# A decode block rebuilt: one load queue, two heads per 4 MB load, a quarter of K on TensorE, the norm folded behind the FFN

## The chip, the cores and the metric

One core of a Trainium2 chip runs the kernel. It has TensorE (PE, matrix products), VectorE (DVE), ScalarE (ACT), GpSimd (POOL) and SyncE (SP), each with an instruction stream of its own, and 16 DMA engines that carry data between HBM and the core's SBUF. TensorE writes to PSUM. A load is issued by an engine's queue; here SP and ACT issue loads. An instruction can wait for semaphores, and whatever stands behind it on that engine waits too. The metric is the device time in microseconds.

## The reference

One token of each of two sequences passes through attention over a cache of 8192 positions with 32 heads of 128, and then through a gated feed-forward part (FFN). Nearly all bytes are K and V: 64 heads of 2 MB each, twice.

```python
B, D, Hq, Sk, Dh, F = 2, 512, 32, 8192, 128, 1376      # all bf16
q = (layernorm(x) @ wq)                                  # per head: 128 values
p = softmax((q . k_cache[b, h]) * Dh ** -0.5)            # 8192 scores per head
o = p @ v_cache[b, h]
h = x + o.reshape(B, 1, Hq * Dh) @ wo
gate, up = layernorm(h) @ W_gate, layernorm(h) @ W_up
out = h + (gate * (gate > 0) * up) @ W_down
```

## The kernel before

A head's K is loaded as `[128 partitions, 64, 128]`: partition p holds the 64 positions 64p to 64p + 63, 16 KB in a row. The loop `for i in range(NH)` runs over the 64 heads; K and V have three buffers each (`kt`, `vt`, `NB = 3`).

For each head VectorE multiplies K by q, which lies copied in all partitions (`prod`, line 327), then adds halves of the 128 products, from 128 to 64, 32, 16 and 8 wide (`tb` and `prod` in turn, line 349), and reduces the last 8 (line 358): 64 scores per partition. ScalarE takes the exponential and its sum (line 363). TensorE multiplies V by the exponentials, 64 matmuls with one column each (line 377). Softmax's division is left to the end.

SP issues the K loads (`dma_k`, line 194), each after the multiply that frees its buffer. ACT issues the V loads (`dma_v`, line 200), each after the PV matmuls that free its buffer. SP's queue also carries x (line 247, in pieces of 2 bytes), wq in eight chunks of 1 KB rows (line 187), wo (behind the K load of head 8, in 1 KB rows), and at the end the FFN's weights into the freed K and V buffers.

q comes in groups of four heads: four matmuls with 512 columns (line 213), whose stationary operand is the normalized x copied along 128 columns, and a copy by ScalarE (line 226).

After the last head comes one chain: the sums of the exponentials (line 399), their reciprocals, spread to all partitions by a matmul (407), the scaling of O (413), the output projection, 128 matmuls (422), the addition of x (427), the second norm with a square root on ScalarE (431 to 453), gate and up (464, 470), their product (475 to 483), W_down (494), the addition, a transpose (506) and the store (511).

Of the kernel before, what the change touches and what calls it, by code (L numbers as in the profile page):

```python
# [6 lines left out]
F32 = mybir.dt.float32  # L7
# [6 lines left out]
class EngChain:  # L14

    def __init__(self, eng, sem):
        self.eng = eng
        self.sem = sem
        self.count = 0
        self.pending = False  # L20

    def wait(self):
        if self.pending:
            self.eng.wait_ge(self.sem, self.count)
            self.pending = False

    def run(self, inst):
        inst.then_inc(self.sem, 1)
        self.count += 1
        self.pending = True  # L30
        return inst


def bass_sequential_preLN__gqa_block_cached__glu_gated_reglu__decode_kernel(
# [13 lines left out]
    _, Hkv, Sk, Dh = A_k_cache.shape  # L48
    Hq = A_wq.shape[1] // Dh
    assert Hq == Hkv  # L50
    assert Dh == 128
    assert D % 128 == 0
    DC = D // 128
    J = Sk // 128
    assert Sk % 128 == 0 and J >= 2 and (J & (J - 1)) == 0
    F = B_W_gate.shape[1]
    FC = (F + 127) // 128
    NH = B * Hq
    inv_sqrt_dh = 1.0 / math.sqrt(Dh)
    eps = 1e-5  # L60
    qdim = Hq * Dh
    GH = 4 if Hq % 4 == 0 else Hq
    NGB = Hq // GH
    NG = B * NGB
    GW = GH * Dh
    assert GW <= 512
    NB = 3

    with ExitStack() as es:
# [3 lines left out]
        sem_x = S("x")  # L73
        sem_wo = S("wo")
        sem_wgu = S("wgu")
        sem_wd = S("wd")
        sem_prep = S("prep")
        sem_stats = S("stats")
        sem_lnx = S("lnx")
        sem_qps = S("qps")  # L80
        sem_qcopied = S("qcopied")
        kdone = [S(f"kdone{k}") for k in range(NB)]
        vdone = [S(f"vdone{k}") for k in range(NB)]
        multdone = S("multdone")
        sready = S("sready")
        expdone = S("expdone")
        pvdone = S("pvdone")
        sem_ident0 = S("ident0")
        sem_ident = S("ident")
        sem_z = S("ztok")  # L90
        sem_zinv = S("zinv")
        sem_zb = S("zb")
        sem_osb = S("osb")
        sem_attn = S("attn")
        sem_hprep = S("hprep")
        sem_hstats = S("hstats")
        sem_hn = S("hn")
        sem_gu = S("gu")
        sem_hd = S("hd")
        sem_y = S("ysem")  # L100
        sem_h2 = S("h2sem")
        sem_rows = S("rowsem")
        sem_rowsb = S("rowsbsem")
        osem = S("osem")
        dvesem = S("dvechain")
        sem_sq1a = S("sq1a")
        sem_sq1b = S("sq1b")
        sem_sq2a = S("sq2a")
        sem_sq2b = S("sq2b")

        dve = EngChain(nc.vector, dvesem)
        actsem = S("actchain")
        actc = EngChain(nc.scalar, actsem)

        kt = [es.enter_context(nc.sbuf_tensor(f"kt{i}", [128, J, Dh], BF16)) for i in range(NB)]
        vt = [es.enter_context(nc.sbuf_tensor(f"vt{i}", [128, J, Dh], BF16)) for i in range(NB)]
        wq_sb = es.enter_context(nc.sbuf_tensor("wq_sb", [128, DC, qdim], BF16))
        xrep = es.enter_context(nc.sbuf_tensor("xrep", [128, B * DC, 128], BF16))
        q_grp = [es.enter_context(nc.sbuf_tensor(f"qgrp{i}", [128, GW], BF16)) for i in range(2)]
        wo_sb = es.enter_context(nc.sbuf_tensor("wo_sb", [128, Hq, D], BF16))  # L120
        ones_f32 = es.enter_context(nc.sbuf_tensor("ones_f32", [128, 128], F32))
        ident_f32 = es.enter_context(nc.sbuf_tensor("ident_f32", [128, 128], F32))
        xT = es.enter_context(nc.sbuf_tensor("xT", [128, DC, B], BF16))
        xT_f = es.enter_context(nc.sbuf_tensor("xT_f", [128, DC * B], F32))
        xsq = es.enter_context(nc.sbuf_tensor("xsq", [128, DC * B], F32))
        sumb = es.enter_context(nc.sbuf_tensor("sumb", [128, B], F32))
        sumq = es.enter_context(nc.sbuf_tensor("sumq", [128, B], F32))
        mean = es.enter_context(nc.sbuf_tensor("mean", [128, B], F32))
        msq = es.enter_context(nc.sbuf_tensor("msq", [128, B], F32))
        var = es.enter_context(nc.sbuf_tensor("var", [128, B], F32))  # L130
        rstd = es.enter_context(nc.sbuf_tensor("rstd", [128, B], F32))
        vareps = es.enter_context(nc.sbuf_tensor("vareps", [128, B], F32))
        sqv = es.enter_context(nc.sbuf_tensor("sqv", [128, B], F32))
        lnxT = es.enter_context(nc.sbuf_tensor("lnxT", [128, DC, B], BF16))
        hT_f = es.enter_context(nc.sbuf_tensor("hT_f", [128, DC * B], F32))
        hsq = es.enter_context(nc.sbuf_tensor("hsq", [128, DC * B], F32))
        hnT = es.enter_context(nc.sbuf_tensor("hnT", [128, DC, B], BF16))
        hd = es.enter_context(nc.sbuf_tensor("hd", [128, FC * B], BF16))
        h2T_f = es.enter_context(nc.sbuf_tensor("h2T_f", [128, DC * B], F32))
        rows_sb = es.enter_context(nc.sbuf_tensor("rows_sb", [DC * B, 128], BF16))  # L140
        zinv = es.enter_context(nc.sbuf_tensor("zinv", [1, NH], F32))
        ZP = es.enter_context(nc.sbuf_tensor("ZP", [128, NH], F32))
        zb_sb = es.enter_context(nc.sbuf_tensor("zb_sb", [128, NH], F32))
        u_sb = es.enter_context(nc.sbuf_tensor("u_sb", [128, FC * B], F32))
        O_sb = es.enter_context(nc.sbuf_tensor("O_sb", [128, Hq, B], BF16))
        prod = es.enter_context(nc.sbuf_tensor("prod", [128, J, Dh], BF16))
        tb1 = es.enter_context(nc.sbuf_tensor("tb1", [128, J * 64], BF16))
        scores = [es.enter_context(nc.sbuf_tensor(f"scores{i}", [128, J], F32)) for i in range(2)]
        e_t = [es.enter_context(nc.sbuf_tensor(f"e{i}", [128, J], BF16)) for i in range(2)]

        if DC * F <= J * Dh and FC * D <= J * Dh and NH >= 3:
            alias_w = True
            pstride = kt[0][:].ap[0]
            wg_view = bass.AP(kt[(NH - 3) % NB], 0, [[pstride[0], 128], [F, DC], [1, F]])
            wu_view = bass.AP(kt[(NH - 2) % NB], 0, [[pstride[0], 128], [F, DC], [1, F]])
            wd_view = bass.AP(vt[(NH - 3) % NB], 0, [[pstride[0], 128], [D, FC], [1, D]])
        else:
            alias_w = False
            wg_t = es.enter_context(nc.sbuf_tensor("wg_sb", [128, DC, F], BF16))
            wu_t = es.enter_context(nc.sbuf_tensor("wu_sb", [128, DC, F], BF16))  # L160
            wd_t = es.enter_context(nc.sbuf_tensor("wd_sb", [128, FC, D], BF16))
            wg_view = wg_t[:]
            wu_view = wu_t[:]
            wd_view = wd_t[:]

        qps = es.enter_context(nc.psum_tensor("qps", [128, 2 * 512], F32))
        work = es.enter_context(nc.psum_tensor("work", [128, 512], F32))
        O_ps = work[:, 0:NH]
        zrow_ps = work[0:1, 64:64 + NH]
        zb_ps = work[:, 128:128 + NH]  # L170
        msum_ps = work[:, 192:192 + DC * B]
        e2_ps = work[:, 200:200 + DC * B]
        attnT_ps = work[:, 208:208 + DC * B]
        hsum_ps = work[:, 216:216 + DC * B]
        hsq_ps = work[:, 224:224 + DC * B]
        g_ps = work[:, 232:232 + FC * B]
        u_ps = work[:, 254:254 + FC * B]
        yT_ps = work[:, 276:276 + DC * B]
        rows_ps = work[0:DC * B, 288:288 + 128]

        NWQ = NGB
        sem_wq = [S(f"wq{k}") for k in range(NWQ)]
        nfull = F // 128
        frem = F - nfull * 128

        def dma_wq_chunk(k):
            return nc.sync.dma_start(  # L187
                wq_sb[:, :, k * GW:(k + 1) * GW],
                A_wq[:, k * GW:(k + 1) * GW].rearrange("(c p) n -> p c n", p=128),
            ).then_inc(sem_wq[k], 16)  # L190

        def dma_k(i):
            b, h = divmod(i, Hq)
            return nc.sync.dma_start(  # L194
                kt[i % NB][:], A_k_cache[b, h].rearrange("(p j) d -> p j d", p=128)
            ).then_inc(kdone[i % NB], 16)

        def dma_v(i):
            b, h = divmod(i, Hq)
            return nc.scalar.dma_start(  # L200
# [3 lines left out]
        def emit_q_group_pe(g):  # L204
# [4 lines left out]
            if g >= 2:  # L209
                nc.tensor.wait_ge(sem_qcopied, g - 1)  # L210
# [335 lines left out]
```

## Time and profile before

| what | value |
|---|---|
| time, median of 3 runs | 710.17 us (710.09 to 710.2) |
| profiled execution: span | 708.4 us |
| first multiply of a head starts | 27.43 us |
| the last head's scores are done | 688.70 us |
| VectorE busy | 630.6 us, 424 instructions |
| TensorE busy | 158.7 us, 4433 matmuls |
| ScalarE busy | 34.4 us |
| read from HBM | 281.05 MB |

The span runs from the first instruction to the last of one profiled execution; the time of a run contains a little more around it. The profile page cuts the span into 40 slices and gives for each the busy tenths of the engines, the share of the 16 DMA engines and the GB/s. Its groups list instructions by line, with the count, the busy time in all, the mean of one in ns, and the idle time before them with what ended it. In an order of time, each line has the start, the duration, the engine, the line and the operation.

### The profile page before, as it was taken

To read this page: it belongs to the slowest core of one execution; us is meant where nothing else is said; L and a number is where in the kernel's file an instruction comes from. 1 tells how busy PE (TensorE), PEld (TensorE's weight loads), DVE (VectorE), ACT (ScalarE), POOL (GpSimd) and SP (SyncE) were. 2 spreads that over 40 slices of the span, in tenths; PEclk is the share of its full clock that TensorE was granted. 3 is DMA by queue.
4 is the path that set the end of the run, shared out by engine and by line. 5 is a ranking of instruction groups with operands and counts; after the bars stand their busy time and mean duration, and the time that the engine had idled before them with its cause. 6 is when DMAs were issued, how large, how long until landed. Compare 5 with 4: busy or idle time off the path is not lost.

```text
span 708.4 us, 9878 instructions
## 1 busy us (share of the span) xinstructions
PE 158.7 (22%) x4433; PEld 130.2 (18%) x4433; DVE 630.6 (89%) x424; ACT 34.4 (5%) x149; POOL 0.7 (0%) x6
## 2 busy tenths in 40 slices
PE   0221322011323132212322132122322232112215
PEld 0111222011222122212221122112221222112215
DVE  0679998299999999999999999999999999999982
ACT  0100000000000000000000000000000000000010
POOL 0000000000000000000000000000000000000000
DMA  9999999999999999999999999999999999999940
GB/s 345 367 426 427 425 417 392 423 396 384 426 424 421 421 418 427 409 409 424 420 425 422 422 413 424 422 412 423 428 427 409 420 424 417 420 417 416 401 162 3
DMA packets 30346, 281.70 MB, mean 398 GB/s; under 512 B 3328, under 2 KB 12896, under 8 KB 13920
## 3 DMA queue, kind: packets, MB, share of 16 engines
q1 hardware_dynamic: 21088, 146.84, 49.9%
q10 hardware_dynamic: 9216, 134.22, 46.1%
q8 instruction: 35, 0.57, 0.3%
q14 instruction: 7, 0.06, 0.0%
HBM read 281.05 MB, written 0.00 MB: 397 GB/s over the span
## 4 chain that ended last, share of the span: by engine, by line
DVE 84%; DMA 8%; SPq 4%; PE 2%; issue 2%; DVEq 0%; ACT 0%
DVE prod L327 38%; DVE tb L349 25%; DVE prod L349 14%; DMA kt<-in_A_k_cache_dram 8%; DVE scores L358 6%; SPq L194 2%; SPq L187 2%; PE work L422 1%; PE work L377 0%; PE work L464 0%; DVEq L323 0%; PE work L470 0%; PE work L494 0%; SPq L247 0%; ACT e L363 0%
## 5 line engine op out<-in xcount | busy, mean ns | idle before, releaser
L327 DVE TENSOR_TENSOR prod<-kt,qgrp 128x8192 bf16<-128x8192 bf16 x64 | 283.3, 4426 | 29.5 <-DMA kt<-in_A_k_cache_dram 20.8
L377 PE MATMUL work<-e,vt 128*128 128x1 bf16 x4096 | 119.5, 165 | 517.7 <-ACT e L363 517.7
L377 PEld LDWEIGHTS work<-e,vt 128*128 128x128 bf16 x4096 | 114.3, 104 | 535.2 <-ACT e L363 535.2
L349 DVE TENSOR_TENSOR tb<-prod 128x4096 bf16<-128x4096 bf16 (+1 forms) x128 | 190.9, 1491 | 4.4
L349 DVE TENSOR_TENSOR prod<-tb 128x2048 bf16<-128x2048 bf16 (+1 forms) x128 | 105.6, 825 | 4.4
L363 ACT ACTIVATE e<-scores 128x64 bf16<-128x64 f32 x64 | 16.4, 256 | 630.8 <-DVE scores L358 630.8
L358 DVE TENSOR_REDUCE scores<-prod 128x64 f32<-128x512 bf16 x64 | 43.9, 686 | 2.2
L213 PE MATMUL qps<-wq_sb,xrep 128*128 128x512 bf16 x64 | 29.9, 623 | 4.4 <-DVEq L303 3.3
L262 DVE CAST xT_f<-xT 128x8 f32<-128x8 bf16 x1 | 0.2, 172 | 19.0 <-DMA xT<-in_A_x_dram 19.0
L363 ACT ACTIVATION_READ_ACCUMULATOR e<-scores 128x1 f32 x64 | 11.9, 186 | 0.0
L213 PEld LDWEIGHTS qps<-wq_sb,xrep 128*128 128x128 bf16 x64 | 6.9, 128 | 14.2 <-issue 8.8
L226 ACT ACTIVATE qgrp<-qps 128x512 bf16<-128x512 f32 x16 | 9.3, 579 | 4.0 <-PE qps L213 4.0
L268 PE MATMUL work<-xT_f,ones_f 128*128 128x8 f32 x2 | 0.6, 372 | 20.4 <-DVE xsq L264 20.4
L268 PEld LDWEIGHTS work<-xT_f,ones_f 128*128 128x128 f32 x2 | 0.5, 310 | 20.4 <-DVE xsq L264 20.4
L422 PE MATMUL work<-O_sb,wo_sb 128*128 128x2 bf16 x128 | 3.6, 165 | 0.6 <-DVEq L416 0.6
L422 PEld LDWEIGHTS work<-O_sb,wo_sb 128*128 128x128 bf16 x128 | 3.5, 104 | 0.8 <-DVEq L416 0.8
L427 DVE TENSOR_TENSOR hT_f<-work,xT_f 128x8 f32<-128x8 f32 x1 | 0.2, 167 | 3.7 <-PE work L422 3.7
L475 DVE COPY u_sb<-work 128x20 f32<-128x20 f32 x1 | 0.2, 178 | 3.1 <-PE work L470 3.1
L403 DVE RECIPROCAL zinv<-work 1x64 f32<-1x64 f32 x1 | 0.5, 547 | 2.6 <-PE work L399 2.6
L464 PE MATMUL work<-hnT,kt 128*128 128x2 bf16 (+1 forms) x44 | 1.5, 170 | 2.1 <-DVEq L457 2.1
L464 PEld LDWEIGHTS work<-hnT,kt 128*128 128x128 bf16 (+1 forms) x44 | 1.5, 112 | 2.2 <-DVEq L457 2.2
L470 PE MATMUL work<-hnT,kt 128*128 128x2 bf16 (+1 forms) x44 | 1.5, 170 | 0.0
(53 smaller groups left out, 21.0 us busy)
## 6 DMA issues: line engine op xcount, KB each, us to landing
vt<-in_A_v_cache_dram ACTq DMA_DIRECT2D x64, 2048.0 KB, 13.0
kt<-in_A_k_cache_dram SPq DMA_DIRECT2D x64, 2048.0 KB, 13.6
wq_sb<-in_A_wq_dram SPq DMA_DIRECT2D x8, 512.0 KB, 11.4
wo_sb<-in_A_wo_dram SPq DMA_DIRECT2D x1, 4096.0 KB, 41.8
kt<-in_B_W_gate_dram SPq DMA_DIRECT2D x1, 1376.0 KB, 10.9
kt<-in_B_W_up_dram SPq DMA_DIRECT2D x1, 1376.0 KB, 6.5
vt<-in_B_W_down_dram SPq DMA_DIRECT2D x1, 1280.0 KB, 9.0
vt<-in_B_W_down_dram SPq DMA_DIRECT2D x1, 96.0 KB, 9.2
```

The costliest lines, as they stand in the source:

```text
L187: return nc.sync.dma_start(wq_sb[:, :, k * GW:(k + 1) * GW], A_wq[:, k * GW:(k + 1) * GW].rearrange("(c p) n -> p c n", p=128),).then_inc( ...
L194: return nc.sync.dma_start(kt[i % NB][:], A_k_cache[b, h].rearrange("(p j) d -> p j d", p=128)).then_inc(kdone[i % NB], 16)
L213: last = nc.tensor.matmul(qps[:, slot * 512:slot * 512 + GW], lhsT=xrep[:, b_g * DC + c, :], rhs=wq_sb[:, c, col0:col0 + GW], start=(c == ...
L226: actc.run(nc.scalar.activation(out=q_grp[slot][:], in_=qps[:, slot * 512:slot * 512 + GW], func=ACT.Copy))
L327: nc.vector.tensor_tensor(out=prod[:], in0=kt[buf][:], in1=qb, op=ALU.mult).then_inc(multdone, 1)
L349: dve.run(nc.vector.tensor_tensor(out=out_ap, in0=cur_in[:, :, 0:half], in1=cur_in[:, :, half:cur_w], op=ALU.add))
L358: nc.vector.tensor_reduce(out=scores[par][:], in_=cur_in, axis=AX.X, op=ALU.add).then_inc(sready, 1)
L363: nc.scalar.activation(out=e_t[par][:], in_=scores[par][:], func=ACT.Exp, scale=inv_sqrt_dh, accum_out=ZP[:, col:col + 1]).then_inc(expdon ...
L377: last = nc.tensor.matmul(O_ps[:, col:col + 1], lhsT=vt[buf][:, j, :], rhs=e_t[par][:, j:j + 1], start=(j == 0), stop=(j == NJ - 1))
L422: last = nc.tensor.matmul(attnT_ps[:, ncx * B:(ncx + 1) * B], lhsT=wo_sb[:, h, ncx * 128:(ncx + 1) * 128], rhs=O_sb[:, h, :], start=(h == ...
L464: last = nc.tensor.matmul(g_ps[0:fw, fc * B:(fc + 1) * B], lhsT=wg_view[:, c, fc * 128:fc * 128 + fw], rhs=hnT[:, c, :], start=(c == 0), s ...
L470: last = nc.tensor.matmul(u_ps[0:fw, fc * B:(fc + 1) * B], lhsT=wu_view[:, c, fc * 128:fc * 128 + fw], rhs=hnT[:, c, :], start=(c == 0), s ...
```

## The change

The kernel's body is written anew; what is computed stays. The parts:

- **Loads.** K and V come two heads at a time (heads 2hp and 2hp + 1 of one sequence), 4 MB each, 32 KB in a row per partition; 64 partitions belong to each head. There are four slots of 4 MB: K in 0 and 2, V in 1 and 3. wq comes whole into slot 3, in 32 KB rows. All loads but x are issued by SP, in one order. wo is issued behind V of pair 16, the FFN's weights go into K's slot of pair 30, ahead of V of pair 31, which comes in four pieces.
- **Scores.** Of a pair's 128 columns, VectorE takes two chunks of 48 in the same way as before. The other 32 are turned by TensorE (four groups of eight transposes), copied to SBUF by ScalarE, and multiplied with q, two columns for the two heads.
- **PV.** 128 matmuls of two columns for a pair: `e_t` has a column for each head, zero in the other head's partitions.
- **q.** 128 matmuls give q with the head's dimension on the partitions; eight rounds of a copy, four matmuls with the identity and a ScalarE copy spread it over the partitions.
- **Output projection.** The sums of the exponentials and the scaling come in batches of pairs 0-7, 8-15, 16-23, 24-30 and 31. 24 heads are projected at pair 27, the rest at the end.
- **Second norm.** Since the gate keeps its sign under a positive factor, `1/(var + eps)` is applied once behind W_down; there is no square root. The output is stored with the partitions outermost.

The removed lines are those of the kernel above. The core of the new ones:

```diff
+    NP = B * H // 2
+    J = 2 * Sk // 128
+    GT = 8
+    NG = 4
+    JP = NG * GT
+    NCH = 2
+    JC = (J - JP) // NCH
...
+        def load(s, dst, src, eng=sp):
+            slot_cnt[s] += 16
+            eng.eng.dma_start(dst, src).then_inc(slot_sem[s], 16)
+            return (slot_sem[s], slot_cnt[s])
+
+        def kv(cache, p):
+            hp, b = divmod(p, B)
+            return cache[b, 2 * hp:2 * hp + 2].rearrange("h (p j) d -> (h p) (j d)", p=64)
...
+                nc.scalar.dma_start(x_row[:], A_x[:, 0]).then_inc(sem_x, 16)
+                t_wq = load(3, slot[3][:], A_wq.rearrange("(p c) n -> p (c n)", c=DC))
+                t_k, t_v = {}, {}
+                t_k[0] = load(0, slot[0][:], kv(A_k_cache, 0))
+                t_v[0] = load(1, slot[1][:], kv(A_v_cache, 0))
+                t_k[1] = load(2, slot[2][:], kv(A_k_cache, 1))
...
+                sp.wait(t_q)
+                t_v[1] = load(3, slot[3][:], kv(A_v_cache, 1))
...
+                def score_group(p, g):
+                    n = p * NG + g
+                    pe.wait(t_ev[n])
+                    if g == 0 and p >= 2:
+                        pe.wait(t_exp[p - 2][0])
+                    for k in range(GT):
+                        jj = g * GT + k
+                        i = nc.tensor.matmul(
+                            Sp[p % 2][:, 2 * jj:2 * jj + 2], lhsT=kT[n % 3][:, k * 128:(k + 1) * 128],
+                            rhs=qT[:, 2 * p:2 * p + 2], start=True, stop=True)
+                    t_sc[n] = pe.run(i)
+
+                def exp(p, k, src, j0, nj):
+                    for a in range(2):
+                        q = slice(64 * a, 64 * a + 64)
+                        t = act.run(nc.scalar.activation(
+                            out=e_t[p % 2][q, j0:j0 + nj, a], in_=src(q, a), func=ACT.Exp, scale=inv_sqrt_dh,
+                            accum_out=zs[q, 2 * p + a, k:k + 1]))
+                    t_exp.setdefault(p, []).append(t)
...
+                for p in range(NP):
...
+                    for c in range(NCH):
+                        dve.wait(t_k[p])
...
+                        t_dm = dve.run(nc.vector.tensor_tensor(
+                            out=prod[:], in0=k_t[:, c * JC:(c + 1) * JC, :], in1=qv, op=ALU.mult))
...
+                        t_s = dve.run(nc.vector.tensor_reduce(out=sc[:], in_=cur, axis=AX.X, op=ALU.add))
+                        if c == 0:
+
+                            pe.wait(t_k[p])
+                            for g in range(NG):
...
+                                for k in range(GT):
+                                    j = NCH * JC + g * GT + k
+                                    i = nc.tensor.transpose(
+                                        Tp[n % 3][:, k * 128:(k + 1) * 128], k_t[:, j, :], ident[:])
+                                t_pt[n] = pe.run(i)
+                                act.wait(t_pt[n])
...
+                                t_ev[n] = act.run(nc.scalar.activation(
+                                    out=kT[n % 3][:], in_=Tp[n % 3][:], func=ACT.Copy))
+                                if g >= 1:
+                                    score_group(p, g - 1)
...
+                    t_kfree[p] = (t_dm, t_pt[p * NG + NG - 1])
...
+                    if p + 2 < NP:
+                        sp.wait(*t_kfree[p])
+                        t_k[p + 2] = load(s, slot[s][:], kv(A_k_cache, p + 2))
...
+                        for j in range(j0, j1):
+                            i = nc.tensor.matmul(
+                                Op[k % 2][:, col:col + 2], lhsT=v_t[:, j, :], rhs=e_t[p % 2][:, j, :],
+                                start=(nmm == 0), stop=(nmm == J - 1))
+                            nmm += 1
+                    t_pv[p] = pe.run(i)
+                    if p + 1 in ends and not last_pair:
+                        t_batch[k] = z_sum(k, *batches[k])
+                        if k < 3:
+                            t_O[k] = normalize(k, *batches[k], t_batch[k], False)
+                    if p + 2 < NP - 1:
+                        sp.wait(t_pv[p])
+                        t_v[p + 2] = load(sv, slot[sv][:], kv(A_v_cache, p + 2))
...
+                        for ci, (j0, j1) in enumerate(((0, 48), (48, 96), (96, 112), (112, 128))):
+                            nc.sync.dma_start(
+                                slot[sl][:, j0 * Dh:j1 * Dh], src[:, j0 * Dh:j1 * Dh]).then_inc(sem_vl[ci], 16)
+                    if p == 14:
+                        nc.sync.dma_start(wo_sb[:], A_wo.rearrange("(h d) n -> d h n", d=128)).then_inc(sem_wo, 16)
+                    if p == 27:
+                        pe.wait((sem_wo, 16), t_O[0], t_O[1], t_O[2])
+                        o_proj(range(0, 24), 0, 2)
...
+                dve.wait(t_var)
+                dve.run(nc.vector.tensor_scalar(
+                    out=vr[:], in0=Sp[0][:, 64:64 + B], scalar1=1.0 / D, scalar2=eps, op0=ALU.mult, op1=ALU.add))
+                dve.last()
+                dve.run(nc.vector.reciprocal(out=r2[:], in_=vr[:]))
```

More of the change, by code (lines that the diff above doesn't have):

```diff
@@ L220, in emit_q_group_copy, with sb @@
[L220 to L229 removed]
+        def sb(name, shape, dt):
+            return es.enter_context(nc.sbuf_tensor(name, shape, dt))
@@ new lines, in _ @@
+                pe.wait(t_O[3])
+                o_proj(range(24, 30), 0, 2)
+                o_proj(range(30, 32), 0, 1)
+                dve.wait(t_pv[NP - 1])
+                t = o_scale(4, 31, 32)
+                pe.wait(t)
+                t = pe.run(o_proj(range(30, 32), 1, 2, last=True))
+                dve.wait(t)
+                t = dve.run(nc.vector.tensor_tensor(out=hb[:], in0=Wp[:, 0:DC * B], in1=xT, op=ALU.add))
+                pe.wait(t)
+                for c in range(DC):
+                    i = nc.tensor.matmul(Sp[0][:, 0:B], lhsT=onesn[:], rhs=hb[:, c * B:(c + 1) * B],
+                                         start=(c == 0), stop=(c == DC - 1))
@@ new lines, in _ @@
+                t_u = ffn_in(Sp[1], wup)
+                t_g = ffn_in(Op[1], wgt)
+                pe.wait(t_d2)
+                for c in range(DC):
+                    i = nc.tensor.matmul(Sp[0][:, 64:64 + B], lhsT=ones_f[:], rhs=d2[:, c * B:(c + 1) * B],
+                                         start=(c == 0), stop=(c == DC - 1))
+                t_var = pe.run(i)
+                dve.wait(t_u)
+                dve.run(nc.vector.tensor_copy(out=u_sb[:], in_=Sp[1][:, 0:FC * B]))
+                dve.last()
```

745 lines of the change are left out of this document (303 added, 442 removed).

## The prediction

> **What bounds the kernel now.** I read the head of the page first: the span, the busy shares and the slices.
>
> ```profile
> span 708.4 us, 9878 instructions
> PE 158.7 (22%) x4433; PEld 130.2 (18%) x4433; DVE 630.6 (89%) x424; ACT 34.4 (5%) x149; POOL 0.7 (0%) x6
> ...
> DMA  9999999999999999999999999999999999999940
> GB/s 345 367 426 427 425 417 392 423 396 384 426 424 421 421 418 427 409 409 424 420 425 422 422 413 424 422 412 423 428 427 409 420 424 417 420 417 416 401 162 3
> ...
> q8 instruction: 35, 0.57, 0.3%
> ...
> HBM read 281.05 MB, written 0.00 MB: 397 GB/s over the span
> ...
> DVE 84%; DMA 8%; SPq 4%; PE 2%; issue 2%; DVEq 0%; ACT 0%
> ```
>
> Two things are nearly full at once: VectorE is busy 89%, and the DMA engines are at 9 in all slices but the last two. The chain that ended last (the last line) lies 84% on VectorE. So I looked at one head, in the groups kept apart by shape and in the order of time:
>
> ```profile
> L327 DVE TENSOR_TENSOR prod<-kt,qgrp 128x8192 bf16<-128x8192 bf16 x64 | 283.3, 4426 | 29.5 <-DMA kt<-in_A_k_cache_dram 20.8 <-ACTq L229 2.8 <-ACT e L363 0.4
> L349 DVE TENSOR_TENSOR tb<-prod 128x4096 bf16<-128x4096 bf16 x64 | 146.7, 2291 | 2.2
> L349 DVE TENSOR_TENSOR prod<-tb 128x2048 bf16<-128x2048 bf16 x64 | 78.4, 1224 | 2.2
> L349 DVE TENSOR_TENSOR tb<-prod 128x1024 bf16<-128x1024 bf16 x64 | 44.2, 691 | 2.2
> L358 DVE TENSOR_REDUCE scores<-prod 128x64 f32<-128x512 bf16 x64 | 43.9, 686 | 2.2
> L349 DVE TENSOR_TENSOR prod<-tb 128x512 bf16<-128x512 bf16 x64 | 27.2, 425 | 2.2
> ```
> ```profile
> 208.13 4.43 DVE L327 TENSOR_TENSOR prod<-kt,qgrp 128x8192 bf16<-128x8192 bf16 x1
> ...
> 218.14 4.43 DVE L327 TENSOR_TENSOR prod<-kt,qgrp 128x8192 bf16<-128x8192 bf16 x1
> ```
>
> The means add to 9.74 us, and the next head starts 10.01 us after the last: VectorE sets the pace, 64 x 10.01 = 640.6 us. A head brings 4.19 MB of K and V, so this pace asks for 419 GB/s. What the DMA engines can do shows in a table of stretches (last two numbers: DMA share, GB/s):
>
> ```profile
> 2.50:4.00 1.50, 0.00 (x0) 0.00 (x0) 0.00 (x0) 0.95 (x1) 0.00 (x0) 1.00 0.60 240
> 4.00:18.00 14.00, 0.00 (x0) 0.00 (x0) 0.00 (x0) 0.00 (x0) 0.00 (x0) 1.00 1.00 401
> 28.00:35.00 7.00, 1.61 (x4) 0.29 (x2) 6.93 (x3) 0.68 (x1) 0.00 (x0) 1.00 1.10 348
> 37.00:41.00 4.00, 3.21 (x68) 2.14 (x68) 0.35 (x1) 0.35 (x2) 0.00 (x0) 1.00 1.00 426
> 40.00:100.00 60.00, 12.45 (x328) 9.48 (x326) 56.98 (x34) 2.71 (x12) 0.00 (x0) 1.00 1.00 426
> 140.00:640.00 500.00, 111.41 (x3213) 92.30 (x3214) 486.53 (x301) 23.73 (x113) 0.00 (x0) 1.00 1.00 418
> 684.00:708.40 24.40, 12.09 (x333) 10.97 (x333) 8.37 (x25) 1.84 (x4) 0.00 (x0) 1.00 0.01 2
> ```
>
> From 40 to 100 us the loads, behind since the start, moved 426 GB/s; later 418, VectorE's pace. From 684 us on nothing is loaded, 24 us in which only the end of the computation runs. The wait for K (total, times, longest) adds the rest:
>
> ```profile
> DVE prod L327 <- DMA kt<-in_A_k_cache_dram: 20.8, 2, 16.5
> ```
>
> The longest, 16.5 us, is the head whose K stood behind the 4 MB of wo in SP's queue. So VectorE's pace is only 2% below what the DMA engines can do: the DMA is the next bound, close behind.
>
> **The change: VectorE leaves the path.** Of the 128 K columns of a pair, 32 go to TensorE; VectorE does two chunks of 48 columns, each 0.75 of a head. By width a chunk is 0.75 x 9.74 + 0.27 for the gaps (10.01 - 9.74) = 7.6 us, a pair 15.2; if nothing scaled, 20.0. A pair's load takes 8.39 MB / 427 GB/s = 19.6 us. I take 15.2, because the rows follow width. At 20.0 it would cost little too: the first multiply at 23 us + 640.6 + the end comes to about the sum below. ScalarE and TensorE take work over; their nearest rows:
>
> ```profile
> L226 ACT ACTIVATE qgrp<-qps 128x512 bf16<-128x512 f32 x16 | 9.3, 579 | 4.0 <-PE qps L213 4.0
> L363 ACT ACTIVATE e<-scores 128x64 bf16<-128x64 f32 x64 | 16.4, 256 | 630.8 <-DVE scores L358 630.8
> L363 ACT ACTIVATION_READ_ACCUMULATOR e<-scores 128x1 f32 x64 | 11.9, 186 | 0.0
> L377 PE MATMUL work<-e,vt 128*128 128x1 bf16 x4096 | 119.5, 165 | 517.7 <-ACT e L363 517.7
> ```
> ```profile
> 24.76 1.89 PE L213 MATMUL qps<-wq_sb,xrep 128*128 128x512 bf16 x4 [3.34 <-DVEq L303]
> ...
> 208.48 1.87 PE L377 MATMUL work<-e,vt 128*128 128x1 bf16 x64 [8.14 <-ACT e L363]
> ```
>
> ScalarE per pair: four evictions of 1024 columns, each between 0.58 and 1.16 us, and six exponentials of 0.44: 5.0 to 7.3 us. TensorE: 160 narrow matmuls (128 for V, 32 scores) at 1.87/64 = 0.029 us, and 32 transposes of 128 columns, each between 0.029 and 0.47 us (1.89/4, a matmul of 512 columns). That is 5.6 to 19.7 us; I take 0.12, a quarter of the 512-column one: 8.5. So I cost both engines at nothing; the cover is the load of the next pair, and what exceeds 19.6 us would be paid 32 times.
>
> **Do the loads ever run dry?** All go through SP's queue now, in the order K, V, K, V. SP waits for the last multiply and the transposes of pair p (about 11 us after K[p] landed) before K[p+2], then for the PV matmuls of p (about 17 us) before V[p+2]; whatever stands behind a waiting load waits too. But K[p+2] is due only when V[p], K[p+1] and V[p+1] have passed, 29 us after K[p] landed, and V[p+2] at 39: 18 and 22 us of slack. V[1] waits for the q matmuls (wq there at 13 us, 128 matmuls 3.6 us) and is due at 42. At the end the weights (issued about 11 us after K[30] landed) go ahead of V[31]; due at 19.6. VectorE is through with K[31] 5 us before V[31] is complete. New waits on VectorE: after pairs 7, 15 and 23 it stands, with the next pair's multiply queued behind, until that pair's last exponentials and PV matmuls are done (0.9 + 48 x 0.029 = 2.3 us), within the 4.4 us that it has to spare; and before the first multiply it awaits eight rounds that spread q over the partitions (13 + 3.7 us, then 8 rounds of about 0.7, an eviction of 0.58 and a hop: 22 us), when K[0] lands at 23. So the stream should not pause, and **the time is: start + stream + what follows the last byte**.
>
> **Stream.** Of 281.05 MB, wo (4.19) and W_down (1.41) still move in 1 KB rows; wq, now in 32 KB rows, leaves that class. The stretch 28:35 is one queue of 1 KB rows: 348 GB/s, so 5.60 MB take 16.1 us. Instruction fetch grows with TensorE's instructions (4433 matmuls to about 6600): 0.57 to 0.85 MB. The rest is 275.45 + 0.85 = 276.3 MB. Is one queue as fast as two? In 37:41 only SP's queue worked:
>
> ```profile
> q1 hardware_dynamic: 119, 1.70, 100.1%
> ```
>
> It made 426 GB/s, as two did. I take 427: **647.1 us**. Longer rows may do a little better: one engine of 16 takes 47.1 ns for 1 KB at 348 and 615.4 ns for 16 KB at 426, so by a straight line 1222 ns for 32 KB, which is 429 GB/s and 643.8 us, an estimate and the lower end. 418 gives 661.0, and 401 (4:18, ACT's queue of V almost alone) 689.0. A rule speaks against it: the Trainium skill, DMA: Bandwidth & Descriptors, Latency and other measured facts, has copies slow down when the rows of the partitions lie at large powers of two (207 GB/s at 512 KiB); here the pitch doubles from 16 to 32 KiB. By 207 the stream would be 1335 us; no run here shows a pitch of 32 KiB, and 16 KiB gave 426.
>
> **Start.** Loads are issued at once; in 2.50:4.00 the rate is 240, a loss of 0.7 us. First byte at 2.5, so 3.2 us. **Uneven finish of the 16 engines:** estimate 1.5 us, between 0.5 and 3, from the flow of the last weights (slices of 0.2 us in 676:684), which falls off over about 1 us:
>
> ```profile
> GB/s 344 413 413 413 427 413 385 440 413 399 399 399 357 378 381 388 384 384 384 394 374 374 358 343 343 353 353 333 348 358 312 277 154 36 20 20 10 0 0 0
> ```
>
> **After the last byte**, from the end of before:
>
> ```profile
> 692.98 0.23 DVE L413 TENSOR_TENSOR O_sb<-work,zb_sb 128x64 bf16<-128x64 f32 x1
> ...
> 696.93 0.17 DVE L427 TENSOR_TENSOR hT_f<-work,xT_f 128x8 f32<-128x8 f32 x1 [3.73 <-PE work L422]
> ...
> 697.35 0.60 PE L431 MATMUL work<-hT_f,ones_f 128*128 128x8 f32 x2 [0.46 <-DVE hsq L429]
> ...
> 697.80 0.57 PE L432 MATMUL work<-hsq,ones_f 128*128 128x8 f32 x2
> ...
> 700.52 1.54 PE L464 MATMUL work<-hnT,kt 128*128 128x2 bf16 x44 [2.15 <-DVEq L457]
> ...
> 703.49 0.18 DVE L475 COPY u_sb<-work 128x20 f32<-128x20 f32 x1 [3.08 <-PE work L470]
> ...
> 704.12 1.33 PE L494 MATMUL work<-hd,vt 128*128 128x2 bf16 x44 [0.67 <-DVEq L487]
> ...
> 706.43 0.65 SPq L511 DMA_DIRECT2D out_dram<-rows_sb  x2
> ```
>
> Last 16 PV matmuls 0.6; scale 0.4; eight matmuls of the projection and the addition 0.6; mean and subtraction 0.5; square and two memsets, which TensorE must await, 0.6; 88 matmuls of gate and up 3.0 (700.52 to 703.49); four f32 matmuls for the variance, at 0.45 as L431 and L432 start apart, 1.7 (but perhaps hidden beside the product on VectorE, then 0); W_down 1.4; two operations for the output 0.4; store 2.0 (706.43 to the end took 2.0; it now has 256 pieces of 8 bytes). For such small pieces the only row is the read of x, 1024 pieces of 2 bytes beside V:
>
> ```profile
> xT<-in_A_x_dram SPq DMA_DIRECT2D x2, 1.0 KB, 18.6
> ```
>
> A quarter of it, 4.7, is the store's upper end. Sum **11.2 us**. The projection of all 32 heads (128 x 0.029 = 3.7), both normalizations and the square root are gone from this part.
>
> 3.2 + 647.1 + 16.1 + 1.5 + 11.2 = 679.1 us of span. The median lies 1.8 us above the profiled span (710.17 against 708.4), so **680.9, in round numbers 681**.
>
> **Rivals.** (1) The same limit, but the stream stays at the 418 GB/s of 140:640: 13.9 us more, 694.8. For it: share 1.00 there too. Against: VectorE asked for no more. (2) Slower than before: a lone stream of 32 KB rows that holds only 401 GB/s, as V did almost alone in 4:18, whether by the queue or by the pitch: 41.9 more, 722.8. It decides at 408 GB/s (276.3 MB in 676.4 us). Against it: 426 in 37:41. The pitch rule of the Trainium skill named above would be one cause. (3) TensorE at its dear end: transposes at 0.47 and the scores at 0.165 us (L377's mean, if none overlaps the next): 24.0 us a pair, 32 x 24.0 + 23 + 13 = 804; it decides at 21 us a pair. Against it: 64 matmuls in 1.87 us. (4) The DMA share of 9 everywhere is already the limit and nothing moves: 708 to 711. Against it: loads end at 684, and 16.5 us were lost in one stall behind wo.
>
> **Chances.** Forecast 0.77, (1) 0.13, (2) 0.05, (3) 0.03, (4) 0.02. The range 673 to 696 holds the forecast with its bounds (low: stream 643.8, finish 0.5, variance hidden and a short store, 8 after the last byte, in all 673) and (1) with a finish of 3 (696); it leaves (2) to (4) out. A measurement here can tell about 0.2% from no change. Faster 0.90, same 0.02, slower 0.08.
>
> **What would show it.** Right: DMA slices of 425 or more up to about 665 us with none falling at pair borders, VectorE at about 470 us busy with a wait for K of about 4 us in each pair, the last wait of the PV matmuls on V's load, and about 11 us after it. Wrong: slices near 400 to 418 at DMA share 1.00 (1 or 2); TensorE or ScalarE without idle time and DMA slices below 9 (3); SP waiting for PV or the multiply while nothing is in flight.

## The result and the profile after

| | before | after |
|---|---|---|
| time, median | 710.18 us (710.09 to 710.4, 4 runs) | 682.79 us (682.76 to 683.07, 4 runs) |
| profiled span | 708.4 us | 680.7 us |
| VectorE busy | 630.6 us | 492.9 us |
| TensorE busy | 158.7 us | 297.6 us |
| ScalarE busy | 34.4 us | 202.6 us |

The ratio is 0.9615, with a 95% interval of 0.9601 to 0.9628: 3.9% faster. The forecast was 681. The head of the page of the kernel after, with the slices, the bytes and the chain:

```profile
PE 297.6 (44%) x6602; PEld 268.7 (39%) x6602; DVE 492.9 (72%) x426; ACT 202.6 (30%) x523; POOL 1.8 (0%) x11
...
PEclk9955566555555555655555556555556555555555
DMA  9999999999999999999999999999999999999990
GB/s 374 437 432 431 428 428 430 430 429 430 432 429 431 430 429 429 430 430 429 430 345 435 429 428 428 428 430 431 428 429 430 429 429 430 430 429 430 409 360 27
...
HBM read 281.05 MB, written 0.00 MB: 413 GB/s over the span
...
DMA 69%; DVE 27%; SPq 2%; PE 1%; issue 1%; DVEq 0%
```

The chain has changed hands: 84% VectorE before, 69% DMA now. The slices mostly stand at 428 to 432, where behind the start they wandered between 384 and 428. Four of the stream fall below 425: the first (374), the one that carries wo (345), and the last two (409, 360). One pair in the order of time, VectorE only, and then all its waits for K in the table of waits (total, times, longest):

```profile
626.39 3.36 DVE L324 TENSOR_TENSOR prod<-slot,q_b 128x6144 bf16<-128x6144 bf16 x1 [4.21 <-DMA slot<-in_A_k_cache_dram]
...
634.14 3.36 DVE L324 TENSOR_TENSOR prod<-slot,q_b 128x6144 bf16<-128x6144 bf16 x1
...
645.83 3.36 DVE L324 TENSOR_TENSOR prod<-slot,q_b 128x6144 bf16<-128x6144 bf16 x1 [3.97 <-DMA slot<-in_A_k_cache_dram]
```
```profile
DVE prod L324 <- DMA slot<-in_A_k_cache_dram: 134.2, 32, 15.6
```

VectorE works 2 x 7.75 = 15.5 us, then waits about 4 us for the next K: 19.4 us a pair, which is 8.39 MB at 432 GB/s. Before, it waited for K twice in the whole run; now it waits in each pair (the longest, 15.6 us, is the K behind wo). Table of stretches of the kernel after (granted TensorE clock, DMA share and GB/s are the last three numbers):

```profile
20.00:28.00 8.00, 5.82 (x64) 4.79 (x64) 5.19 (x5) 5.14 (x9) 0.00 (x0) 1.00 0.98 422
100.00:300.00 200.00, 87.27 (x1929) 78.89 (x1930) 152.16 (x124) 61.03 (x160) 0.00 (x0) 0.53 1.00 430
620.00:640.00 20.00, 8.69 (x192) 7.84 (x192) 15.41 (x13) 6.13 (x16) 0.00 (x0) 0.50 1.00 421
640.00:668.00 28.00, 10.79 (x234) 9.79 (x235) 17.69 (x21) 6.80 (x20) 0.00 (x0) 0.50 0.83 330
...
650.00:653.00 3.00, 1.07 (x19) 0.64 (x17) 2.86 (x5) 2.15 (x6) 0.00 (x0) 0.50 0.56 202
664.00:668.00 4.00, 2.56 (x90) 2.39 (x88) 0.00 (x0) 0.00 (x0) 0.00 (x0) 0.50 0.23 89
```

The row 640:668 is the weak place: 330 GB/s at a DMA share of 0.83. The two rows below it show where it falls: a hole from 650 to 653 us, and the last 4 us, in which the engines finish unevenly. The order of time shows what happens there, and after it:

```profile
639.48 11.62 SPq L384 DMA_DIRECT2D wd_last<-in_B_W_down_dram  x1
...
651.14 2.02 SPq L426 DMA_DIRECT2D slot<-in_A_v_cache_dram  x4
...
661.92 0.26 ACT L261 ACTIVATE e<-scores 64x48 bf16<-64x48 f32 x1 [7.65 <-DVE scores L339]
...
667.84 0.59 PE L407 MATMUL O<-e,slot 128*128 128x2 bf16 x16 [0.62 <-DMA slot<-in_A_v_cache_dram]
...
668.28 1.48 PE L303 MATMUL W<-O_sb,wo_sb 128*128 128x2 bf16 x40
...
673.72 1.84 PE L482 MATMUL S<-d,ones_f 128*128 128x2 f32 x8
...
677.52 0.40 SPq L513 DMA_DIRECT2D out_dram<-o_c  x1
```

SP's instruction that issues the small rest of W_down takes 11.62 us. The 1280 rows of W_down stand before it in the same queue, and V[31] stands behind it: its four pieces are issued at 651.14 us only, in the middle of the hole. The last PV matmuls then wait for V[31] until 667.84, though the exponentials were ready at 662.6.

### The profile page after: what moved, and what is told of

It reads as the page before. It is cut to its first block, busy times and chain, and to the rows that moved or that the text cites. A ratio compares the mean times of both kernels' runs of the same rounds, so it can differ in the third digit from the quotient of the medians.

```text
span 680.7 us, 14440 instructions
## 1 busy us (share of the span) xinstructions
PE 297.6 (44%) x6602; PEld 268.7 (39%) x6602; DVE 492.9 (72%) x426; ACT 202.6 (30%) x523; POOL 1.8 (0%) x11
## 4 chain that ended last, share of the span: by engine, by line
DMA 69%; DVE 27%; SPq 2%; PE 1%; issue 1%; DVEq 0%
DMA slot<-in_A_k_cache_dram 66%; DVE prod L324 16%; DVE tb L332 6%; DVE prod L332 3%; DMA slot<-in_A_v_cache_dram 2%; SPq L384 2%; DVE scores L339 1%; PE S L482 0%; PE S L473 0%; PE O L501 0%; PE O L473 0%; PE W L303 0%; SPq L426 0%; SPq L133 0%; SPq L379 0%
## 5 line engine op out<-in xcount | busy, mean ns | idle before, releaser
L324 DVE TENSOR_TENSOR prod<-slot,q_b 128x6144 bf16<-128x6144 bf16 x64 | 214.9, 3358 | 135.3 <-DMA slot<-in_A_k_cache_dram 134.2
L407 PE MATMUL O<-e,slot 128*128 128x2 bf16 x4096 | 119.5, 165 | 248.4 <-ACT e L261 124.2
L407 PEld LDWEIGHTS O<-e,slot 128*128 128x128 bf16 x4096 | 114.4, 104 | 253.6 <-DMA slot<-in_A_v_cache_dram 126.9
L355 ACT ACTIVATE kT<-T 128x1024 bf16<-128x1024 bf16 x128 | 126.9, 1022 | 171.7 <-PE T L349 170.7
L349 PE MATMUL T<-ident,slot 128*128 128x128 bf16 x1024 | 123.6, 307 | 71.9 <-DMA slot<-in_A_k_cache_dram 71.9
L332 DVE TENSOR_TENSOR tb<-prod 128x3072 bf16<-128x3072 bf16 (+1 forms) x128 | 148.2, 1158 | 4.4
L349 PEld LDWEIGHTS T<-ident,slot 128*128 128x128 bf16 x1024 | 100.3, 141 | 74.9 <-DMA slot<-in_A_k_cache_dram 74.9
L332 DVE TENSOR_TENSOR prod<-tb 128x1536 bf16<-128x1536 bf16 (+1 forms) x128 | 84.2, 658 | 4.4
L253 PE MATMUL S<-qT,kT 128*128 128x2 bf16 x1024 | 48.4, 168 | 33.0 <-ACT kT L355 31.7
L253 PEld LDWEIGHTS S<-qT,kT 128*128 128x128 bf16 x1024 | 41.1, 107 | 52.0 <-ACT kT L355 52.0
L261 ACT ACTIVATION_READ_ACCUMULATOR e<-S 64x1 f32 x64 | 12.9, 201 | 0.7
L235 ACT ACTIVATE q_b<-O 128x512 bf16<-128x512 f32 x8 | 4.3, 594 | 15.6 <-PE O L230 15.6
```

The lines of the kernel that those rows point to most:

```text
L235: t_cp[m] = act.run(nc.scalar.activation(out=q_b[:, m * 512:(m + 1) * 512], in_=Op[m % 2][:], func=ACT.Copy))
L253: i = nc.tensor.matmul(Sp[p % 2][:, 2 * jj:2 * jj + 2], lhsT=kT[n % 3][:, k * 128:(k + 1) * 128], rhs=qT[:, 2 * p:2 * p + 2], start=True, ...
L261: t = act.run(nc.scalar.activation(out=e_t[p % 2][q, j0:j0 + nj, a], in_=src(q, a), func=ACT.Exp, scale=inv_sqrt_dh, accum_out=zs[q, 2 * p ...
L324: t_dm = dve.run(nc.vector.tensor_tensor(out=prod[:], in0=k_t[:, c * JC:(c + 1) * JC, :], in1=qv, op=ALU.mult))
L332: dve.run(nc.vector.tensor_tensor(out=o, in0=cur[:, :, 0:half], in1=cur[:, :, half:w], op=ALU.add))
L349: i = nc.tensor.transpose(Tp[n % 3][:, k * 128:(k + 1) * 128], k_t[:, j, :], ident[:])
```

## The experiments

Theory: the time is that of one unbroken stream of loads plus what stands ahead of its first and behind its last byte; VectorE had only to fall below the 19.5 us that a pair's load takes. Rivals: VectorE's work sets the time in proportion; the single queue itself raises the rate; TensorE's slower clock or the longer rows matter. All ratios below are to the kernel before; the edits are cut to their main lines.

**All of K back on VectorE**

```diff
-    NG = 4
+    NG = 0
...
-                            score_group(p, NG - 1)
-                            act.wait(t_sc[p * NG + NG - 1], t_const)
+                            act.wait(t_const)
```

> All 128 columns of K on VectorE (two chunks of 64), nothing on TensorE; loads, queue and end as after the change. Theory (the loads set the time, VectorE had to be lowered only below 19.5 us a pair): VectorE needs 20.0 us a pair, 0.5 above the loads, and its three waits for the batches' sums (8.3 us in all after the change) are no longer hidden: first multiply 24.0 + 32 x 20.0 + 8.3 = 672 us, then the last exponentials and PV matmuls 2.8 and the end 12.3: span 688, time 690. Rival (the gain came from taking K off VectorE): VectorE is back at its old work and so is the time, 705 to 712. Rival (a slower clock of TensorE because of the transposes costs time): TensorE's clock goes back to 1.0 and the time falls below 683.

Measured: 694.7 us, ratio 0.9783 (0.977 to 0.9796). The waits of its VectorE:

```profile
DVE zr L279 <- PE O L271: 9.6, 3, 3.2
...
DVE prod L324 <- DMA slot<-in_A_k_cache_dram: 2.3, 1, 2.3
```

VectorE waits for K only once, ahead of the first pair: it is the bound again, at 4425 ns a multiply as before. Still 15.5 us of the 27.4 remain. In the spans (708.4 to 692.5): the first multiply comes 3.6 us earlier (23.83 against 27.43), and the waits for K after it are gone (4.26 + 16.53 = 20.8); the three waits for the batches' sums give back 9.6 and their small instructions more, so that the last scores come at 675.03 instead of 688.70; the end behind them is 2.2 us shorter. So the part on TensorE is worth 11.9 us, and the rest of the rewrite, its loads above all, 15.5. (The 11.9 us are counted with the new loads in place; the 15.5 us were read off the traces, not taken apart by runs.) The theory was 4.7 us low: the last pair's PV matmuls all stand behind its sum on TensorE and take 3.55 us, where 2.8 had been set for them and the exponentials together, and each batch costs VectorE its own operations too.

**Half of TensorE's share**

```diff
-    NG = 4
+    NG = 2
```

> TensorE takes 16 of the 128 columns instead of 32, VectorE two chunks of 56. Theory (loads set the time): VectorE 17.8 us a pair, still below 19.5, so the time stays: 682.8 within 0.3%. Rival (time follows VectorE's work): 32 x 2.4 us more, up to 760; rival (TensorE or ScalarE hold the pairs up): faster than 681.

Measured: 682.12 us, ratio 0.9604 (0.9591 to 0.9617). VectorE does a sixth more and the time stays (0.7 us less). From its page:

```profile
PE 221.3 (33%) x5578; PEld 202.6 (30%) x5578; DVE 563.8 (83%) x426; ACT 137.2 (20%) x459; POOL 1.7 (0%) x11
```

Neither VectorE's 71 us more nor the 76 us less on TensorE show in the time. Here the granted clock of TensorE was 1.00 throughout, after the change about 0.5: the clock costs no more than these 0.7 us either.

**V on ScalarE's queue again**

```diff
-                        sp.wait(t_pv[p])
-                        t_v[p + 2] = load(sv, slot[sv][:], kv(A_v_cache, p + 2))
+                        act.wait(t_pv[p])
+                        t_v[p + 2] = load(sv, slot[sv][:], kv(A_v_cache, p + 2), act)
```

> V is loaded by ScalarE's queue again, K by SP's; sizes and all else as after the change. Theory (bytes per row length set the rate, the queue does not): 683, within 4 us, DMA slices of 428 to 430. Rival (the single queue is what raised the rate from 418 to 430): slices near 418, the stream 18 us longer, 697 to 702.

Measured: 690.47 us, ratio 0.9719 (0.9705 to 0.9732). Neither expectation was right: most slices are as high as with one queue, yet 7.7 us are lost.

```profile
GB/s 383 437 399 420 427 429 427 429 429 436 429 429 430 428 432 426 428 433 429 428 395 406 424 256 427 448 426 429 426 425 441 426 430 431 427 429 434 350 406 38
```
```profile
654.89 3.36 DVE L324 TENSOR_TENSOR prod<-slot,q_b 128x6144 bf16<-128x6144 bf16 x1
```

One slice falls to 256 (about 395 to 412 us), after VectorE had waited 29.6 us for the K that stood behind wo; and VectorE begins the last pair at 654.89, 9 us later than after the change. My first reading was that wo alone does it.

**Two queues, wo first**

```diff
+                nc.sync.dma_start(wo_sb[:], A_wo.rearrange("(h d) n -> d h n", d=128)).then_inc(sem_wo, 16)
                 t_k, t_v = {}, {}
...
-                    if p == 14:
-                        nc.sync.dma_start(wo_sb[:], A_wo.rearrange("(h d) n -> d h n", d=128)).then_inc(sem_wo, 16)
```

> As the run with two queues (V on ScalarE's queue), but wo is loaded first behind wq instead of in the middle. Theory (two queues are as fast as one; the 7.7 us were lost because K alone stood behind wo, V ran ahead, and later the DMA engines stood idle for some 5 us): no slice in the middle falls below 420, and the time is 683 to 686. Rival (two queues lose bandwidth all along): 690 as with wo in the middle.

Measured: 689.46 us, ratio 0.9711 (0.9698 to 0.9724). That reading falls: the hole in the middle is gone, the time is not. The slices of this run, VectorE's first and last pair, and two stretches near the start:

```profile
GB/s 383 411 394 308 425 425 434 435 432 431 426 428 430 433 428 432 431 426 432 435 425 426 429 435 430 434 427 428 428 427 435 430 425 435 426 425 425 284 407 37
```
```profile
55.33 3.36 DVE L325 TENSOR_TENSOR prod<-slot,q_b 128x6144 bf16<-128x6144 bf16 x1 [26.43 <-DMA slot<-in_A_k_cache_dram]
...
654.45 3.36 DVE L325 TENSOR_TENSOR prod<-slot,q_b 128x6144 bf16<-128x6144 bf16 x1
```
```profile
62.00:66.00 4.00, 2.36 (x80) 2.30 (x80) 3.90 (x4) 1.38 (x9) 0.00 (x0) 0.55 0.09 33
60.00:70.00 10.00, 2.92 (x96) 2.69 (x94) 9.69 (x10) 3.36 (x10) 0.00 (x0) 0.62 0.58 215
```

From 70 to 630 us the rate is that of one queue, but the last pair begins at 654.45 again. Each K shares the DMA engines with its own V and lands with it, where one queue in the order K, V lets K land half a pair earlier. What VectorE does with the last K then no longer lies beside the last loads, which shows as 284 in the third slice from the end: V[31] and the weights can't be asked for yet. That was the new theory, and the next run its test.

It left out the fourth slice (308), where most of the loss lies. At the start V runs ahead on its own queue: V[0] and V[1] land at 22.7 and 39.6 us, while K[0] stands behind wq and wo, so VectorE begins the first pair at 55.33 us only. By 62 us 25.0 MB have moved, which is wq, wo, K[0], V[0], K[1] and V[1]: all four slots are full and none is free, and for 4 us nearly nothing moves. At 430 GB/s the stretch from 60 to 70 us lacks 5.0 us. The low slice of the run before is the same: VectorE, late behind wo, began again at 391.95, the loads stood still from 400 to 404 us (4 GB/s), and the next K was asked for at 403.08, behind that pair's second multiply.

**Two queues, wo first, the first V behind the first K**

```diff
-                t_v[0] = load(1, slot[1][:], kv(A_v_cache, 0), act)
...
-                act.wait(t_q)
-                t_v[1] = load(3, slot[3][:], kv(A_v_cache, 1), act)
...
+                act.wait(t_k[0], t_q)
+                t_v[0] = load(1, slot[1][:], kv(A_v_cache, 0), act)
+                t_v[1] = load(3, slot[3][:], kv(A_v_cache, 1), act)
```

> As the run with two queues and wo first, but the first V is asked for only when the first K has landed, so that each K shares the DMA engines with the V of the pair before and not with its own. Theory (the runs with two queues lose nothing in GB/s; sharing makes each K land half a pair later against its V, so VectorE begins the last pair at about 654 instead of 646 us, and that is the loss): K[31] lands at 646 to 648 again, the time is 682 to 685. Rival (two queues cost 7 us in whatever order): 689 to 690.

Measured: 683.46 us, ratio 0.9613 (0.96 to 0.9626), the same as one queue (its runs lie between 681.64 and 683.94). The first pair begins at 36.19, the last at 646.98, and the stretch from 60 to 70 us is full:

```profile
36.19 3.36 DVE L325 TENSOR_TENSOR prod<-slot,q_b 128x6144 bf16<-128x6144 bf16 x1 [14.53 <-DMA slot<-in_A_k_cache_dram]
...
646.98 3.36 DVE L325 TENSOR_TENSOR prod<-slot,q_b 128x6144 bf16<-128x6144 bf16 x1
```
```profile
60.00:70.00 10.00, 8.37 (x192) 7.68 (x192) 7.26 (x6) 4.34 (x6) 0.00 (x0) 1.00 0.98 418
```

Of the 6.0 us between the two runs, 4.7 lie in this stretch. The third slice from the end is low here too (322 against 284), which makes about 1.5 us. So the order is what counts, as the theory had it, but mostly because V ran ahead of K at the start and the loads then paused, and less by where the last K lands. One queue is worth nothing in GB/s; it is worth its order. (wo comes first in both runs; one queue with wo first was not run.) This agrees with the Trainium skill, DMA: Bandwidth & Descriptors, Issuing engines are not separate DMA queues: whatever engine issues them, loads run on the same 16 DMA engines.

**Rows of 16 KB**

```diff
-            slot_cnt[s] += 16
-            eng.eng.dma_start(dst, src).then_inc(slot_sem[s], 16)
+            for h in range(2):
+                slot_cnt[s] += 16
+                w = slice(h * SLOT // 2, (h + 1) * SLOT // 2)
+                eng.eng.dma_start(dst[:, w], src[:, w]).then_inc(slot_sem[s], 16)
```

> Each 4 MB load is split into two of 2 MB with 16 KB rows, on the same queue, the partitions still 32 KB apart in HBM. Theory (each row costs an engine a fixed 9 ns beside its bytes): 426 instead of 430 GB/s on 272.6 MB, 6 us more: 688 to 689. Rival (row length is nothing, one queue is enough): 683. Rival (a pitch of 32 KB costs something, long rows hide it): slices below 420, above 695.

Measured: 687.78 us, ratio 0.9685 (0.9672 to 0.9698), 5.0 us above the kernel after. The slices:

```profile
GB/s 371 431 426 427 425 427 426 427 426 426 426 426 427 426 425 429 426 427 425 427 356 427 426 426 426 428 428 426 426 426 427 426 426 427 425 426 426 411 354 25
```

426 instead of 430: the rate that 16 KB rows had in the kernel before. 6 us more had been expected. The number of loads doubles too, which this run doesn't separate from the row length. The partitions lie 32 KB apart here as in the kernel after; neither shows a loss by that.

**W_down behind the last V**

```diff
-                        nc.sync.dma_start(wd_last[0:FR, :], B_W_down[1280:F]).then_inc(sem_w, 16)
...
                                 slot[sl][:, j0 * Dh:j1 * Dh], src[:, j0 * Dh:j1 * Dh]).then_inc(sem_vl[ci], 16)
+                        nc.sync.dma_start(
+                            slot[ws][:, 2 * DC * F:2 * DC * F + 10 * D].rearrange("p (r n) -> p r n", n=D),
+                            B_W_down[0:1280].rearrange("(r p) n -> p r n", p=128)).then_inc(sem_wdl, 16)
+                        nc.sync.dma_start(wd_last[0:FR, :], B_W_down[1280:F]).then_inc(sem_wdl, 16)
```

> W_down is issued behind the last V instead of ahead of it; nothing else changes. Theory: the last load on the path is V[31], which now is through 4 us of W_down and 1 to 2 us of a hole earlier, at about 662.5 instead of 667.8 us; then the last exponentials (662.6) and 128 PV matmuls (3.7) end the pair at about 666.4 instead of 668.4, and W_down lands beside the tail: 2.0 us less, 680.8. Rival (any order of the last loads gives the same end of the stream, and so the same time): 682.8. Rival (SP stands still at another load then): 682 or more, a hole stays in the last slices.

Measured: 681.1 us, ratio 0.9593 (0.9579 to 0.9606), 1.7 us less. V[31] is issued at 638.76 instead of 651.14, and the stretch from 650 to 653 us moves 425 GB/s instead of 202: the hole is gone. The matmuls of the last pair now run in one go behind VectorE:

```profile
662.93 3.55 PE L403 MATMUL O<-e,slot 128*128 128x2 bf16 x128
```

**A shorter tail.** The variance's operands are bf16 here (the squares are rounded), in the next two runs too.

```diff
-                pe.wait(t_O[3])
-                o_proj(range(24, 30), 0, 2)
-                o_proj(range(30, 32), 0, 1)
...
                         normalize(4, 31, 32, zt, True)
+                        pe.wait(t_O[3])
+                        o_proj(range(24, 30), 0, 2)
+                        o_proj(range(30, 32), 0, 1)
...
-        d2 = sb("d2", [128, DC * B], F32)
+        d2 = sb("d2", [128, DC * B], BF16)
```

> 32 of the 40 last projection matmuls go ahead of the last pair's PV matmuls, and the variance is summed with bf16 operands instead of f32 (the squares are rounded to bf16). Theory (what follows the last byte is on the path in full): 32 x 0.029 = 0.9 us and 1.7 - 0.3 = 1.4 us less: 680.5. Rival (the variance is hidden beside the product on VectorE): 681.9.

Measured: 680.71 us, ratio 0.9588 (0.9575 to 0.9601), 2.1 us less where 2.3 had been worked out: what follows the last byte counts nearly in full.

**Both, and the last pair's matmuls in the order of readiness** (V[31] comes in three pieces in that order)

```diff
-                        order = [(1, 0, 48), (2, 48, 96), (0, 96, 112), (0, 112, 128)]
+                        order = [(1, 0, 48), (0, 96, 128), (2, 48, 96)]
...
+                        if last_pair and ci == 2:
...
+                            zt = z_sum(4, 31, 32)
+                            normalize(4, 31, 32, zt, True)
```

> Both edits of the other two runs, and in the last pair the PV matmuls that wait for VectorE's second chunk come last, with its sum just before them (V[31] in three pieces in that order). Theory: the path at the end is K[31] at 645.8, VectorE 16.1, exponentials 0.5, sum 0.5, 48 PV matmuls 1.4, then 10.4 of tail: 674.7 us of span, 677 of time. Rival (the end of the stream holds the end whatever the order): 680 to 681.

Measured: 677.39 us, ratio 0.9542 (0.9529 to 0.9555), 5.4 us less than the kernel after: the two edits alone gave 1.7 and 2.1, so 1.6 come with the order of readiness.

**K[31] ahead of V[30], V[31] ahead of the weights**

```diff
+                    if p == NP - 3:
+                        sp.wait(t_pv[p - 1])
+                        t_v[p + 1] = load((2 * p + 3) % 4, slot[(2 * p + 3) % 4][:], kv(A_v_cache, p + 1))
...
-                    if p + 2 < NP - 1:
+                    if p + 2 < NP - 2:
```

> As the version with both edits at the end, and K[31] is loaded ahead of V[30], and V[31] ahead of all FFN weights. Theory: VectorE goes from pair 30 to pair 31 without a wait, its last scores come at about 657 instead of 661; V[31] lands at 656, gate and up at 662, W_down at 667; then the FFN waits for gate and up, and W_down for its load: 672 us of span, 674 of time. Rival (the last weights, now behind everything, hold the end): 677 or more.

Measured: **675.17 us**, ratio 0.9506 (0.9493 to 0.9519): the fastest version, 1.1% below the kernel after. VectorE goes from pair 30 to the last pair without a wait. Its two multiplies there, and the first of W_down's matmuls:

```profile
641.96 3.36 DVE L324 TENSOR_TENSOR prod<-slot,q_b 128x6144 bf16<-128x6144 bf16 x1
...
650.68 3.36 DVE L324 TENSOR_TENSOR prod<-slot,q_b 128x6144 bf16<-128x6144 bf16 x1
```
```profile
667.60 0.46 PE L505 MATMUL O<-hd,slot 128*128 128x2 bf16 x10 [0.39 <-DVE vr L496]
```

The table names VectorE as what these matmuls waited for. But the last piece of W_down, issued at 639.25, landed 28.2 us later, at 667.45, and VectorE's product was done at 667.39: the two come together, and the load holds the matmuls up by some 0.15 us (they start 0.39 us behind the product's start, 0.23 in the run before).

## Why the prediction was right, point by point

- **VectorE leaves the path: right.** 15.5 us a pair where 15.2 were worked out: a multiply of 6144 took 3.36 us, not 0.75 x 4.43 = 3.32. (Its busy time, 492.9 us, is above the 470 given as a sign.) The run with 16 columns on TensorE shows that the work on it is free up to the load's 19.5 us, and the run with none that beyond this it counts at once. That run also refutes the aside that a pair of 20.0 us would cost little: it cost 11.9, because the three waits for the batches' sums (9.6) are no longer covered and the last PV matmuls stand behind VectorE.
- **ScalarE and TensorE are covered: right.** An eviction took 1022 ns (between 0.58 and 1.16 was given), 16 transposes 1.89 us, which is 0.12 each, as taken.
- **Stream: the mechanism was right; that the sum put the last byte at 667.9 us and it came at 667.8 is luck,** for several sizes were off and cancelled. The rate was 430 GB/s, not 427: 276.3 MB take 642.6 us, 4.5 less; the straight line had said 429. The start cost 1.8 us instead of 3.2 (351 GB/s over the first 10 us). Against these, the stretch with wo (377 GB/s from 335 to 362 us) took 1.0 more than its rows were priced at, and "the stream should not pause" failed at the end. In 640:668 9.24 MB moved; W_down in 4.05 us and the rest at 430 would have taken 22.3, so 5.7 us were lost where 1.5 were set down for the uneven finish. 1.6 of them lie in the hole from 650 to 653 us. The step missed that an issue instruction can itself hold SP (11.62 us), so that V[31] was asked for too late. 3.2 lie in the last 4 us: the uneven finish itself, above the 3 that was its upper bound. The last 0.9 are spread between.
- **Which loads matter at the end** was not asked. The three runs on the end's order show that it was worth 5 us and more: 1.7 for W_down behind V[31], 1.6 for the order of readiness, 2.2 for K[31] ahead of V[30] and V[31] ahead of the weights.
- **After the last byte: 12.9 us, not 11.2.** Two terms were too small, the others 0.4 us too large in all. Of 40 projection matmuls the sum had only eight on the path, but the other 32 stand behind the last PV matmuls in TensorE's order (0.9). The store took 3.2 us, not 2.0 (677.52 to the end), within its bounds; by the Trainium skill, DMA: Bandwidth & Descriptors, Specifications, transfers below 512 B do not reach line rate, which goes with 8-byte pieces, though no run here separates it.
- **Outside the span**: 2.1 us in the profiled run, and 1.8 in the other three, as taken.
- **Rivals.** (1) the rate of 418 did not stay; it fits VectorE's demand, 419. (2) a lone stream at 401 did not come; the same stretch, 4:18, moved 421 after the change. The large pitch that the Trainium skill warns of (DMA: Bandwidth & Descriptors, Latency and other measured facts; its figures start at 512 KiB) shows nothing at 32 KB: 430. (3) is refuted by the transposes at 0.12 us, (4) by the time.
- **Not asked in the prediction: what the single queue is worth.** It was counted as free. It is, in GB/s; its order K before V is worth 6.7 to 7.7 us against two queues that share, mostly because VectorE, kept waiting for a K at the start or behind wo, finds all slots full and the loads pause.

## What to carry to other kernels

When an engine runs at nearly the pace of the DMA, work taken off it is worth only what it was slower than the loads (here 11.9 of 27.4 us): price the time as bytes by the rate of their row length, plus what stands ahead of the first byte and behind the last, and look for what breaks the stream. With two loads per step, let the one that starts the longer computation go first, above all at the start: where the other runs ahead of it, the computation begins late, and the loads stand still once all buffers are full. At the end, order the loads by how much work hangs behind each, and put loads of many short rows behind all others in a queue.

## What the runs showed of the hardware

- The granted clock of TensorE, as the profile has it, fell to 0.5 after the change and cost nothing that the times show. The two rows of 16 transposes, in stretches of clock 1.00 and 0.50 (quoted above), are equally long, and in both ScalarE's first eviction starts 1.07 us behind their start (25.14 and 627.49):

```profile
24.07 1.89 PE L349 MATMUL T<-ident,slot 128*128 128x128 bf16 x16 [1.44 <-DMA slot<-in_A_k_cache_dram]
...
626.42 1.89 PE L349 MATMUL T<-ident,slot 128*128 128x128 bf16 x16 [2.01 <-DMA slot<-in_A_k_cache_dram]
```

The Trainium skill, TensorE: Matmul & The Clock Gate, Part 1: The HAM clock gate, has two clocks, half and full, and puts the half one down to idle stretches. The values agree; the cause doesn't: with half the transposes, or none, TensorE was idle for longer and the clock stayed at 1.00. What lowers it here stays open.
- One DMA issue held SP for 11.62 us (20.43 in the version with both edits) when 1280 rows of 1 KB stood before it in the queue, and the K load behind wo's 4096 such rows held it for 25.36 (18.84 and 37.99 for K[0] in the runs with wo first), where the other issues of 4 MB in 128 rows take 0.33 to 0.53. That the many rows ahead are the reason is argued from this, not tried by itself.
- The rate by row length: 348 GB/s at 1 KB, 426 at 16 KB, 430 at 32 KB on one queue, and for 32 KB rows the same on two (429 and 430 from 68 to 630 us).
- When the last short rows run, the rate stays for some microseconds at about half (172 to 255 GB/s in steps of 1 us from 660 to 665 us, in the runs with W_down last), as if half of the DMA engines were through earlier. Why they drift apart was not tried.
